# Issuing two weight loads from GpSimd, and taking the attention output's product out of PSUM

## The chip, the cores and the metric

The kernel runs on one core of a Trainium2 chip. The core has a matrix engine (TensorE, "PE" in the profile, with its weight loads as "PEld"), three elementwise engines (VectorE "DVE", ScalarE "ACT", GpSimd "POOL"), a SyncE ("SP") that here only issues DMAs, and 16 DMA engines. Each engine runs its own instructions in the order in which they were issued and waits on semaphores for the others. The metric is the device time of one execution in microseconds (us), and lower is better.

## The reference

Attention over 8 batches, 12 heads, 448 positions and 64 values a head, with normed q and k, and then a gated MLP that mixes over positions:

```python
q_n, k_n = rmsnorm(q, g_q), rmsnorm(k, g_k)
scores = scale * q_n @ k_n.T
attn = exp(scores - max) / (sum(exp) + 1e-09)
x = (attn @ v) laid out as (8, 448, 768)

h = gelu(x @ w_in)                      # w_in is 768 x 1024
u, v = halves of h
v_n = layernorm(v) * g_ln
v_s = w_sg @ v_n + b_sg                 # w_sg is 448 x 448
out = x + (u * v_s) @ w_out             # w_out is 512 x 768
```

w_in and w_out come as 64-bit floats, and the kernel reads their two 32-bit words and builds 32-bit floats out of them on the chip. Most products are done as three 16-bit matmuls: a value is split into a high half (its rounding to f16) and a low half (what is left), and high x high, high x low and low x high are added up. The low half of a value is always "the value minus its high half", so it needs one elementwise subtraction.

## The kernel before

**The order is a plan.** The kernel isn't issued as it is written. Each engine call is recorded as a task on a tape (lines 201 to 232), and a list scheduler (lines 255 to 414) runs through modelled time and puts the tasks into an order for each engine by priority, readiness and modelled cost (lines 135 to 173). A task recorded with `either` (lines 234 to 243) names several engines that could do it; the plan gives it to the one that by its model ends it first (`best`, lines 245 to 253). VectorE and GpSimd share a port to SBUF; the model calls every GpSimd task a user of that port, and of VectorE's tasks those that touch SBUF alone (lines 175 to 182). When the order is written out (`emit`), a GpSimd task of a modelled cost over `LONG` = 500 ns is ordered behind the last VectorE task that used the port (lines 440 to 443). PSUM has eight banks; the plan gives a tile a bank and frees it when the last user of the tile has ended (lines 391 to 396), with at most two of the kind "pv" at once (line 42). All recorded instructions have line 439 in the profile, so they are told apart by their tiles.

**Attention.** 48 pairs of heads are done in 24 units `u` of two pairs (four heads). For a unit, q and k are loaded by four DMAs from SP (`load_qk`), squared and summed (`squares`), normed (`norms`, small GpSimd instructions), scaled and split into halves (`split`, GpSimd by default: products into `qk`, differences into `hl`), and turned by two transposing DMAs from SP into `qt`. `scores` does seven row blocks: matmuls into `s`, a minimum on VectorE (`jk`), an exponential on ScalarE (`ex`), two instructions that take the halves of the exponential apart (`ahl`), and a transposing DMA from SP into `at`. `pv` (lines 873 to 904) multiplies with v in two parts, `e` = 0 of 512 columns and `e` = 1 of 384: 48 parts in all. Small GpSimd instructions (`rx`, `rh`, `rl`) prepare the reciprocals of the sums; matmuls lay them out as `row` in PSUM, ScalarE copies that to SBUF, and the part ends with the lines that the change touches:

```python
894  V.tensor_tensor(out=ps, in0=ps, in1=row, op=ALU.mult)   # in PSUM, in place
899  copy(xh, ps, XH)                                        # ScalarE, high half
900  V.tensor_tensor(out=xl, in0=ps, in1=xh, op=ALU.subtract) # VectorE, low half
```

So the PSUM tile `pv` is held until the low half is done. `xh` and `xl` are the x that the MLP's matmuls (`mv`, `mu`, and the addition of x in `mo`) read.

**Weights.** `weights` (lines 591 to 689) runs beside the first units. It loads w_in in 12 chunks of 512 KB into `raw` (three buffers, line 606), decodes each with five VectorE instructions into `dec` (lines 584 to 589), and loads a further chunk when a buffer comes free, so up to three ahead. The first chunk has no other wait; the others also wait for the task that `HOLD` names (lines 1145 and 1146). After six chunks the half of w_in is scaled and split into `wi`. Then come w_sg (`wsr`), and w_out in 8 chunks of 384 KB into `rawo` (two buffers, line 673), decoded into `wr` and split into `wo_h` and `wo_l`. All these loads are issued by SP, in one queue with the transposes.

**MLP.** `moe(b)` runs one batch behind attention at a lower priority; the first needs w_in, w_sg and w_out, so the MLP of batch 0 can only end when `weights` has.

Of the kernel before, what the change touches and what calls it, by code (L numbers as in the profile page):

```python
# [8 lines left out]
F32 = mybir.dt.float32  # L9
# [6 lines left out]
ALU = mybir.AluOpType  # L16
# [29 lines left out]
NAT, NAH, NQT, NVH, HLB, GV = 2, 3, 2, 4, 3, 3  # L46
NOT, NX, NEX = 2, 6, 2
EXP_SET = "natural_log_exp_and_others"
BACC_KW = dict(dynamic_dma_scratch_size=1024)
# [54 lines left out]
class Tape:  # L104
# [30 lines left out]
    def cost(self, q, op, a, kw):  # L135
# [15 lines left out]
        if q.eng != "S" and "dma" in op:  # L151
            return 700, 4000, None
        if q.eng == "S":
# [47 lines left out]
    def record(self, q, op, a, kw):  # L201
# [11 lines left out]
        self.count += 1  # L213
        if q.eng == "S":
            t.preds |= self.after
# [231 lines left out]
def kernel(  # L447
# [75 lines left out]
    mm = T.matmul  # L523
    ENG = dict(A=A, V=V, G=G)

    def copy(out, in_, on):
# [11 lines left out]
    def two(out, in0, in1, op, on):  # L538
        tape.either(*[(ENG[e], "tensor_tensor", dict(out=out, in0=in0, in1=in1, op=op)) for e in on])

    SSW = 2 * C7
# [38 lines left out]
    def decode(dst, raw, most=None):  # L580

        hi, lo = raw[:, :, 1], raw[:, :, 0]
        di = dst.bitcast(I32)
        V.tensor_scalar(out=di, in0=hi, scalar1=0x7FFFFFFF, scalar2=None, op0=ALU.bitwise_and)
        more = {} if most is None else dict(op1=ALU.max, accum_out=most)
        V.tensor_scalar(out=dst, in0=dst, scalar1=LEAST, scalar2=None, op0=ALU.max, **more)
        V.tensor_scalar(out=di, in0=di, scalar1=3, scalar2=0x3FFFFFF8, op0=ALU.logical_shift_left, op1=ALU.bitwise_and)
        V.scalar_tensor_tensor(out=di, in0=hi, scalar=-0x40000000, in1=di, op0=ALU.bitwise_and, op1=ALU.bitwise_or)
        V.scalar_tensor_tensor(out=di, in0=lo, scalar=29, in1=di, op0=ALU.logical_shift_right, op1=ALU.bitwise_or)

    def weights():
# [10 lines left out]
        def load_raw(j):  # L602
            if j < len(chunks):
                x, t = chunks[j]
                held, tape.after = tape.after, set() if j < RAWF else tape.after
                raws[j] = stage.tile([P, DH, 2], I32, name="raw", bufs=RAWB)
                SP.dma_start(out=raws[j].rearrange("p a b -> p (a b)"),
                             in_=wi_b[t * P:(t + 1) * P, x * 2 * DH:(x + 1) * 2 * DH])
                tape.after = held
# [3 lines left out]
        for x in (1, 0):  # L613
# [13 lines left out]
            for t in range(KT):  # L627
                wh, wl = (wi[:, t, x, n] for n in range(2))
                A.activation(out=wh, in_=dec[t], func=AF.Copy, scale=wsc)
                V.scalar_tensor_tensor(out=wl, in0=dec[t], scalar=wsc, in1=wh, op0=ALU.mult, op1=ALU.subtract)  # L630
                if t % 2:
                    yield
# [8 lines left out]
        for s_ in range(C7):  # L641
            SP.dma_start(out=wsr[s_ // 2][s_ % 2 * HP:(s_ % 2 + 1) * HP],
                              in_=w_sg.rearrange("(p c) s -> c p s", c=C7)[s_])
# [27 lines left out]
        for j in range(2 * FT):  # L671
            t, es = j // 2, slice(j % 2 * EH, (j % 2 + 1) * EH)
            raw = mlp.tile([P, EH, 2], I32, name="rawo", tag="v" + "hl"[j % 2])
            SP.dma_start(out=raw.rearrange("p a b -> p (a b)"),
                         in_=wo_b[t * P:(t + 1) * P, 2 * EH * (j % 2):2 * EH * (j % 2 + 1)])
            wr = mlp.tile([P, EH], F32, name="wr", tag="gt", bufs=NOT)
            decode(wr, raw)
            A.activation(out=wo_h[:, t, es], in_=wr, func=AF.Copy)
            V.tensor_tensor(out=wo_l[:, t, es], in0=wr, in1=wo_h[:, t, es].bitcast(F32), op=ALU.subtract)
            yield  # L680
# [19 lines left out]
    def load_qk(u, qs=None):  # L700
        if u >= NI // NG:
            return
        qs = qs or [SP]
        b, h0 = u // NU, u % NU * 2 * NG
# [10 lines left out]
    def load_v(i):  # L715
# [9 lines left out]
        for h, half, s0, c0, n in ((0, lo, 0, 0, C4), (0, hi, 0, C4, CM), (1, lo, C4, C4, CM), (1, hi, CM, 0, C4)):  # L725
            SP.dma_start(out=vp[half, :, s0 * D:(s0 + n) * D], in_=src[h][:, :, c0 * D:(c0 + n) * D])
        for j in range(GV):
# [69 lines left out]
    def vsplit(i):  # L797
# [5 lines left out]
        A.activation(out=vf, in_=vr, func=AF.Copy, scale=sc)  # L803
        V.scalar_tensor_tensor(out=vl.rearrange("p c d -> p (c d)"), in0=vr, scalar=sc, in1=vf, op0=ALU.mult, op1=ALU.subtract)
        r.update(vh=vh, vl=vl)
# [51 lines left out]
    def rows(e, rh, rl):  # L857
# [7 lines left out]
        if ROWP:  # L865
            return ps
        row = att.tile([P, C4 * P], F32, name="row", bufs=1)[:, 0:n * P]
        scaled(row, ps, 2.0 ** -25, RW)
# [4 lines left out]
    def pv(u, e):  # L873
# [18 lines left out]
        if ROWP:  # L892
            row = rows(e, *r_)
        V.tensor_tensor(out=ps, in0=ps, in1=row, op=ALU.mult)
        if e == 0:
# [3 lines left out]
        copy(xh, ps, XH)  # L899
        V.tensor_tensor(out=xl, in0=ps, in1=xh, op=ALU.subtract)  # L900
        if e == 1:
# [18 lines left out]
    def moe(b, early=False):  # L920
# [151 lines left out]
        for t in range(CM + b % 2):  # L1072
# [28 lines left out]
            for h in range(2):  # L1101
                SP.dma_start(out=om[b % 2, 2 * t + h] if t < CM else om[h, C7 - 1], in_=ot[h * HP:(h + 1) * HP])
        if b % 2 == 1:
# [145 lines left out]
```

## Time and profile before

| | us |
|---|---|
| median of 3 runs (lowest, highest) | 860.91 (857.09, 862.02) |
| the profiled execution's own time | 860.37 |
| its span, first to last instruction | 858.6 |
| outside the span | 1.8 |
| busy in the span: TensorE | 743.0 |
| busy: ScalarE | 722.3 |
| busy: VectorE | 668.2 |
| busy: GpSimd | 304.5 |

The profile shows one execution. "Busy" is the time with an instruction on the engine; an engine idle before an instruction has the instruction or the DMA that released it named. A page shows the span in 40 equal slices (21.5 us each) with a digit for the busy tenths; the view by windows gives the same in us for chosen stretches. The view of waits adds up who waited for whom. The chain is the work that ended last, followed back from the last instruction.

### The profile page before, as it was taken

To read this page: it belongs to the slowest core of one execution; us is meant where nothing else is said; L and a number is where in the kernel's file an instruction comes from. 1 tells how busy PE (TensorE), PEld (TensorE's weight loads), DVE (VectorE), ACT (ScalarE), POOL (GpSimd) and SP (SyncE) were. 2 spreads that over 40 slices of the span, in tenths; PEclk is the share of its full clock that TensorE was granted. 3 is DMA by queue.
4 is the path that set the end of the run, shared out by engine and by line. 5 is a ranking of instruction groups with operands and counts; after the bars stand their busy time and mean duration, and the time that the engine had idled before them with its cause. 6 is when DMAs were issued, how large, how long until landed. Compare 5 with 4: busy or idle time off the path is not lost.

```text
span 858.6 us, 21024 instructions
## 1 busy us (share of the span) xinstructions
PE 743.0 (87%) x7766; PEld 475.1 (55%) x7766; DVE 668.2 (78%) x1691; ACT 722.3 (84%) x1495; POOL 304.5 (35%) x457
## 2 busy tenths in 40 slices
PE   0445568954999979999999999999999999999997
PEld 0223343532675548655765568556855686558557
DVE  6978988889988878977976898878987978574250
ACT  4677879998898999898989999889999999895451
POOL 2543350045534634452444246323435335000000
PEclk9658668966999999999999999999999999999999
DMA  6999999969999998999699979997999699646002
GB/s 165 252 241 195 216 207 199 213 141 200 169 234 218 226 190 166 246 209 166 137 206 225 226 145 226 240 209 134 198 225 218 140 223 200 136 90 143 19 1 74
DMA packets 433944, 155.97 MB, mean 182 GB/s; under 512 B 402545, under 2 KB 427697, under 8 KB 433841
## 3 DMA queue, kind: packets, MB, share of 16 engines
q1 hardware_dynamic: 433840, 154.63, 89.6%
q8 instruction: 61, 1.00, 0.5%
q14 instruction: 43, 0.34, 0.1%
HBM read 43.57 MB, written 11.01 MB: 64 GB/s over the span
## 4 chain that ended last, share of the span: by engine, by line
PE 55%; ACT 17%; DVE 12%; DMA 9%; issue 5%; POOL 1%; SPq 1%; ACTq 0%; DVEq 0%; POOLq 0%
PE pv L439 11%; PE s L439 7%; DMA at<-ahl 6%; ACT ex L439 4%; ACT ahl L439 3%; DVE jk L439 2%; ACT L439 2%; ACT sqk L439 2%; PE row L439 1%; DVE ahl L439 1%; DMA qk<-in_k_dram 1%; ACT vg L439 1%; ACT u L439 1%; ACT vh L439 1%; DVE pv L439 1%
## 5 line engine op out<-in xcount | busy, mean ns | idle before, releaser
L439 DVE TENSOR_SCALAR_CACHE_REDUCE jk<-s 128x448 bf16<-128x448 f32 x336 | 199.0, 615 | 34.8 <-PE s L439 34.4
L439 ACT ACTIVATE ex<-s,nm 128x448 int32<-128x448 f32 x336 | 213.6, 641 | 12.1 <-DVE jk L439 9.8
L439 ACT ACTIVATE ahl<-ex 128x896 f16<-128x896 uint16 x192 | 181.9, 957 | 9.5 <-DMA at<-ahl 8.9
L439 PE MATMUL s<-qt 64*64 64x448 f16 x2016 | 142.8, 375 | 48.4 <-DMA qt<-hl 21.3
L439 PEld LDWEIGHTS <-vh 128*64 128x64 f16 (+2 forms) x1792 | 103.2, 112 | 103.6 <-issue 55.7
L439 PE MATMUL pv<-at,vh 128*64 128x192 f16 (+3 forms) x1536 | 133.0, 275 | 27.6 <-ACT ex L439 12.3
L439 DVE TENSOR_SCALAR ahl<-ex 128x896 f16<-128x896 uint16 x144 | 102.5, 712 | 28.8 <-ACT ex L439 22.7
L439 PEld LDWEIGHTS <-qt 64*64 64x64 f16 x2016 | 64.7, 110 | 94.4 <-issue 52.5
L439 POOL TENSOR_TENSOR hl<-qk,hl 128x896 f16<-128x896 f32 (+2 forms) x69 | 93.7, 1364 | 41.7 <-ACT hl L439 9.7
L439 PEld LDWEIGHTS <-wi 128*128 128x128 f16 x576 | 54.5, 99 | 55.5 <-issue 7.2
L439 POOL TENSOR_TENSOR qk<-qk,ny 128x896 f32<-128x896 f32 x46 | 77.1, 1690 | 14.5 <-DVE ahl L439 7.5
L439 POOL TENSOR_TENSOR qk<-qk,gg 128x896 f32<-128x896 f32 x23 | 48.1, 2093 | 96.0 <-ACT sqk L439 77.4
L439 PEld LDWEIGHTS <-xh 128*128 128x128 f16 (+1 forms) x648 | 49.7, 102 | 47.7 <-issue 20.8
L439 PE MATMUL pv<-at,vl 128*64 128x192 f16 (+3 forms) x768 | 74.0, 273 | 0.0
L439 ACT ACTIVATION_READ_ACCUMULATOR ex<-s,nm 128x1 f32 x336 | 71.6, 213 | 0.0
L439 POOL TENSOR_SCALAR rx<-sums 128x8 f32<-128x8 f32 (+1 forms) x48 | 15.0, 313 | 141.8 <-ACT ex L439 140.3
L439 PEld LDWEIGHTS <-vl 128*64 128x64 f16 (+2 forms) x896 | 56.1, 114 | 12.8 <-issue 0.7
L439 DVE TENSOR_REDUCE ss<-sqk 128x14 f32<-128x896 f32 x48 | 51.8, 1079 | 10.2 <-ACT sqk L439 10.1
L439 DVE TENSOR_TENSOR pv<-pv,row 128x512 f32<-128x512 f32 (+1 forms) x48 | 30.2, 629 | 34.3 <-PE pv L439 34.1
L439 ACT ACTIVATE sqk<-qk 128x896 f32<-128x896 f32 x48 | 45.8, 960 | 3.4 <-DMA qk<-in_k_dram 1.8
L439 PEld LDWEIGHTS <-xl 128*128 128x128 f16 (+1 forms) x408 | 36.6, 102 | 19.5 <-DVE v_i L439 1.1
L439 ACT ACTIVATE xh<-pv 128x512 f16<-128x512 f32 (+1 forms) x48 | 26.2, 547 | 24.4 <-DVE pv L439 23.7
(1104 smaller groups left out, 1799.7 us busy)
## 6 DMA issues: line engine op xcount, KB each, us to landing
qk<-in_q_dram SPq DMA_DIRECT2D x48, 224.0 KB, 3.9
qk<-in_k_dram SPq DMA_DIRECT2D x48, 224.0 KB, 4.7
out_dram<-ot SPq DMA_DIRECT2D x56, 192.0 KB, 3.4
raw<-in_moe_w_in_dram SPq DMA_DIRECT2D x12, 512.0 KB, 5.4
vr<-in_v_dram SPq DMA_DIRECT2D x32, 192.0 KB, 4.2
vr<-in_v_dram SPq DMA_DIRECT2D x32, 144.0 KB, 3.7
rawo<-in_moe_w_out_dram SPq DMA_DIRECT2D x8, 384.0 KB, 3.6
at<-ahl SPq DMA_TRANSPOSE x168, 4.6
```

The costliest lines, as they stand in the source:

```text
L439: ins = getattr(q.nc_eng, op)(*first, *a, **kw)
```

## The change

Two things change, and the rest of the diff gives names to choices that keep their old values (`DEC`, `VL`, `WL`, `SQ_`, `VQ`, `KQ`, `XQ` leave their instructions where they were).

First, the 12 loads of w_in and the 8 of w_out are issued by GpSimd's queue instead of SP's. The plan's model takes a DMA on GpSimd as 1100 ns of GpSimd (it had 700, which nothing used) and 4000 ns until it lands, and such a DMA heeds the hold as SP's do.

Second, the product of the attention output goes to a new SBUF tile `sx`, which shares its two buffers with `row` (that had one). The high half is copied from there, and the subtraction for the low half reads SBUF alone, so that GpSimd can do it as well: the plan picks VectorE or GpSimd.

```diff
+DEC, XL, VL, WL = 'V', 'VG', 'V', 'V'
+RQ, OQ, SQ_, VQ, GLAT, KQ, XQ = 'G', 'G', 'S', 'S', (1100, 4000), 'S', 'S'
...
         if q.eng != "S" and "dma" in op:
-            return 700, 4000, None
+            return *GLAT, None
...
-        if q.eng == "S":
+        if "dma" in op:
             t.preds |= self.after
...
+    LD = dict(S=SP, G=G, A=A)
...
+    def stt(out, in0, by, in1, op0, op1, on):
+        tape.either(*[(ENG[e], "scalar_tensor_tensor", dict(out=out, in0=in0, scalar=by, in1=in1, op0=op0, op1=op1)) for e in on])
...
                 raws[j] = stage.tile([P, DH, 2], I32, name="raw", bufs=RAWB)
-                SP.dma_start(out=raws[j].rearrange("p a b -> p (a b)"),
+                LD[RQ].dma_start(out=raws[j].rearrange("p a b -> p (a b)"),
...
             raw = mlp.tile([P, EH, 2], I32, name="rawo", tag="v" + "hl"[j % 2])
-            SP.dma_start(out=raw.rearrange("p a b -> p (a b)"),
+            LD[OQ].dma_start(out=raw.rearrange("p a b -> p (a b)"),
...
-        row = att.tile([P, C4 * P], F32, name="row", bufs=1)[:, 0:n * P]
+        row = att.tile([P, C4 * P], F32, name="row", bufs=2 if "G" in XL else 1)[:, 0:n * P]
...
-        V.tensor_tensor(out=ps, in0=ps, in1=row, op=ALU.mult)
+        if "G" in XL:
+            sx = att.tile([P, C4 * P], F32, name="sx", tag="row", bufs=2)[:, 0:n * P]
+            V.tensor_tensor(out=sx, in0=ps, in1=row, op=ALU.mult)
+            ps = sx
+        else:
+            V.tensor_tensor(out=ps, in0=ps, in1=row, op=ALU.mult)
...
         copy(xh, ps, XH)
-        V.tensor_tensor(out=xl, in0=ps, in1=xh, op=ALU.subtract)
+        two(xl, ps, xh, ALU.subtract, XL)
```

`two` (lines 538 and 539) is `either` over the named engines with one `tensor_tensor`. Since the plan is made anew, the order of everything behind these edits may differ too.

More of the change, by code (lines that the diff above doesn't have):

```diff
@@ L588, in decode @@
         V.scalar_tensor_tensor(out=di, in0=hi, scalar=-0x40000000, in1=di, op0=ALU.bitwise_and, op1=ALU.bitwise_or)
-        V.scalar_tensor_tensor(out=di, in0=lo, scalar=29, in1=di, op0=ALU.logical_shift_right, op1=ALU.bitwise_or)
+        stt(di, lo, 29, di, ALU.logical_shift_right, ALU.bitwise_or, DEC)
     def weights():
@@ L629, in weights @@
                 A.activation(out=wh, in_=dec[t], func=AF.Copy, scale=wsc)
-                V.scalar_tensor_tensor(out=wl, in0=dec[t], scalar=wsc, in1=wh, op0=ALU.mult, op1=ALU.subtract)
+                stt(wl, dec[t], wsc, wh, ALU.mult, ALU.subtract, WL)
                 if t % 2:
@@ L641, in weights @@
         for s_ in range(C7):
-            SP.dma_start(out=wsr[s_ // 2][s_ % 2 * HP:(s_ % 2 + 1) * HP],
+            LD[SQ_].dma_start(out=wsr[s_ // 2][s_ % 2 * HP:(s_ % 2 + 1) * HP],
                               in_=w_sg.rearrange("(p c) s -> c p s", c=C7)[s_])
@@ L702, in load_qk @@
             return
-        qs = qs or [SP]
+        qs = qs or [LD[KQ if u else "S"]]
         b, h0 = u // NU, u % NU * 2 * NG
@@ L725, in load_v @@
         for h, half, s0, c0, n in ((0, lo, 0, 0, C4), (0, hi, 0, C4, CM), (1, lo, C4, C4, CM), (1, hi, CM, 0, C4)):
-            SP.dma_start(out=vp[half, :, s0 * D:(s0 + n) * D], in_=src[h][:, :, c0 * D:(c0 + n) * D])
+            LD[VQ].dma_start(out=vp[half, :, s0 * D:(s0 + n) * D], in_=src[h][:, :, c0 * D:(c0 + n) * D])
         for j in range(GV):
@@ L803, in vsplit @@
         A.activation(out=vf, in_=vr, func=AF.Copy, scale=sc)
-        V.scalar_tensor_tensor(out=vl.rearrange("p c d -> p (c d)"), in0=vr, scalar=sc, in1=vf, op0=ALU.mult, op1=ALU.subtract)
+        stt(vl.rearrange("p c d -> p (c d)"), vr, sc, vf, ALU.mult, ALU.subtract, VL)
         r.update(vh=vh, vl=vl)
@@ L1101, in moe @@
             for h in range(2):
-                SP.dma_start(out=om[b % 2, 2 * t + h] if t < CM else om[h, C7 - 1], in_=ot[h * HP:(h + 1) * HP])
+                LD[XQ if b < B - 1 else "S"].dma_start(out=om[b % 2, 2 * t + h] if t < CM else om[h, C7 - 1], in_=ot[h * HP:(h + 1) * HP])
         if b % 2 == 1:
```

## The prediction

> **What bounds the kernel now.** I read the engines' totals and the slices first, then two windows, then the waits of TensorE.
>
> ```profile
> PE 743.0 (87%) x7766; PEld 475.1 (55%) x7766; DVE 668.2 (78%) x1691; ACT 722.3 (84%) x1495; POOL 304.5 (35%) x457
> ...
> PE   0445568954999979999999999999999999999997
> ...
> DVE  6978988889988878977976898878987978574250
> ...
> PEclk9658668966999999999999999999999999999999
> ```
>
> The slices show two regimes. In the first ten (0 to 215 us) TensorE is half idle, its granted clock is low, and VectorE is the fullest engine. From then on TensorE is full to the end. The windows give that in us (columns: window, length, then busy us and instructions of PE, PEld, DVE, ACT and POOL, granted clock, DMA share, GB/s):
>
> ```profile
> 0.00:210.00 210.00, 111.11 (x1138) 63.45 (x1140) 177.33 (x438) 166.49 (x327) 77.20 (x114) 0.75 0.94 203
> 210.00:859.00 649.00, 631.90 (x6636) 411.68 (x6628) 490.82 (x1253) 555.83 (x1169) 227.31 (x343) 0.99 0.89 175
> ```
>
> TensorE idles 210 - 111.1 = 98.9 us before 210 us and only 649 - 631.9 = 17.1 us after. So an edit pays in the first window, where it lets work reach TensorE sooner, and afterwards by at most what it takes out of 17.1 us. VectorE is 177.3 / 210 = 84% busy in the first window and the DMA engines 94%: two candidates for what paces it. The chain of waits through the first 215 us mixes them:
>
> ```profile
> by line: DMA at<-ahl 12.1%; PE pv L439 11.3%; issue 8.7%; ACT ahl L439 8.1%; ACT ex L439 5.8%; DMA qk<-in_k_dram 4.4%; DVE dec L439 3.5%; ACT sqk L439 3.5%; DVE jk L439 3.5%; SPq L439 3.1%; ACT L439 3.0%; DMA qt<-hl 2.9%; PE s L439 2.2%; AC
> ```
>
> No engine holds it alone; the transposes `at<-ahl` are its largest single item, 12.1% of 215 us = 26 us.
>
> **The change part by part.** I work from the profiled execution, 858.6 us of span and 1.8 around it, 860.4 in all; the median shown is 0.5 above.
>
> *The low half.* The first window holds eight of the 48 subtractions:
>
> ```profile
> L439 DVE TENSOR_TENSOR xl<-pv,xh 128x512 f16<-128x512 f32 x4 | 2.7, 687 | 0.0
> ...
> L439 DVE TENSOR_TENSOR xl<-pv,xh 128x384 f16<-128x384 f32 x4 | 2.2, 553 | 0.7 <-ACT xh L439 0.7
> ```
>
> That is 4.9 us of VectorE. The model makes GpSimd's version about twice as dear (1162 against 602 ns for 512 columns by lines 169 and 173), so the plan gives it away only when over half a us of work stands ahead on VectorE. At 84% load I take five of eight, worth 5 x 0.62 = 3.1 us. Bounds: nothing, if VectorE isn't what is late, and 4.9. On GpSimd the nearest instructions are subtractions of the same shapes:
>
> ```profile
> 29.75 1.15 POOL L439 TENSOR_TENSOR hl<-qk,hl 128x512 f16<-128x512 f32 x1 [0.35 <-POOL hl L439]
> 31.47 0.92 POOL L439 TENSOR_TENSOR hl<-qk,hl 128x384 f16<-128x384 f32 x1 [0.56 <-DVE ahl L439]
> ```
>
> So a moved one ends about 0.45 us later for the matmuls that read it, and GpSimd gets some 5 us in a window where it idles 210 - 77 = 133. It adds waits: the moved subtraction sits behind VectorE's last port user, and behind it on GpSimd stand the norms and reciprocals; and the product of the next part needs the buffer of `sx`. How far apart are the parts?
>
> ```profile
> L439 DVE TENSOR_TENSOR pv<-pv,row x48: 550/626/700, 62.7 to 801.6; 128x512 f32<-128x512 f32 x24, 128x384 f32<-128x384 f32 x24
> ```
>
> 48 products (durations least, median and most in ns) in 739 us, 15 us apart on the mean, which covers the second wait; without that cover `jk` would queue behind a product on VectorE. After 210 us VectorE is 491 of 649 us busy with TensorE full, so the other 40 subtractions cost and bring nothing.
>
> *The bank.* `pv` is now free when the product is done, and no longer after the high and low halves. Where did TensorE wait for a low half?
>
> ```profile
> PE ms__4409 L439 <- DVE xl L439: 4.8, 1, 4.8
> ...
> PE mo__7939 L439 <- DVE xl L439: 0.8, 1, 0.8
> ...
> PE s L439 <- DVE xl L439: 0.3, 1, 0.3
> PE mv__898 L439 <- DVE xl L439: 0.2, 1, 0.2
> ```
>
> 6.1 us in all. The long one, at 303 us, reads no x (`ms` multiplies w_sg), so it waited for the bank:
>
> ```profile
> 302.74 0.70 DVE L439 TENSOR_TENSOR pv<-pv,row 128x512 f32<-128x512 f32 x1
> ...
> 305.39 1.63 DVE L439 TENSOR_TENSOR vl<-vg,vh 128x512 f16<-128x512 f32 x3 [1.43 <-ACT vh L439]
> 306.09 0.58 ACT L439 ACTIVATE xh<-pv 128x512 f16<-128x512 f32 x1
> ...
> 306.94 0.68 DVE L439 TENSOR_TENSOR xl<-pv,xh 128x512 f16<-128x512 f32 x1
> ```
>
> The product ended at 303.4, the low half at 307.6. With the bank gone at 303.4, what is late next is the rest of `vl`, ready at 307.0: TensorE could start `ms` but soon runs out. I take 3 us for the part; bounds 0 (a new plan may place a like wait elsewhere) and 6.1. The high half now reads SBUF instead of PSUM:
>
> ```profile
> 63.47 0.60 ACT L439 ACTIVATE xh<-pv 128x512 f16<-128x512 f32 x1 [2.64 <-DVE pv L439]
> ...
> 217.30 0.62 ACT L439 ACTIVATE hl<-qk 128x512 f16<-128x512 f32 x1
> ```
>
> The second is the same copy out of SBUF: 0.02 us more, 48 times, is 1 us of ScalarE over the run, which I cost at nothing under TensorE; if it all showed, 1 us.
>
> *SP's queue.* Twenty loads leave it. They cost it 12 x 0.53 and 8 x 0.47 = 10.1 us of issue, and waits for their buffers at its head:
>
> ```profile
> L439 SPq DMA_DIRECT2D raw<-in_moe_w_in_dram x12: 327/532/1240, 7.2 to 99.9; - x12
> ...
> L439 SPq DMA_DIRECT2D rawo<-in_moe_w_out_dram x8: 333/468/582, 150.2 to 198.2; - x8
> ...
> SPq L439 <- DVE dec L439: 6.0, 5, 2.6
> ...
> SPq L439 <- DVE wr L439: 5.4, 5, 1.9
> ```
>
> Behind them stood transposes. Two show it on the chain:
>
> ```profile
> 62.07 3.50 SPq L439 DMA_DIRECT2D raw<-in_moe_w_in_dram  x2
> 65.63 2.28 SPq L439 DMA_TRANSPOSE at<-ahl  x1
> ...
> at<-ahl SPq DMA_TRANSPOSE x168, 4.6
> ...
> qt<-hl SPq DMA_TRANSPOSE x48, 4.4
> ...
> 29.43 6.32 DMA qt<-hl
> ...
> 65.63 7.83 DMA at<-ahl
> ```
>
> Against the medians these were 7.83 - 4.6 = 3.2 and 6.32 - 4.4 = 1.9 us late, each with loads of `raw` just ahead. The bytes still cross the same 16 engines, so I take 2 us of 5.1, with 0 and 5.1 as bounds.
>
> *GpSimd's queue.* An issue on GpSimd is in no row. Below stands 0, since it can hide in 133 us of idle time; above, GpSimd's longest regular instruction, 2.08 us (below), for each of 20, that is 42. I take 0.53, as on SP, and hide it. Not hidden is the first chunk: it has no wait, and on GpSimd it can start before q and k of unit 0 have landed, where SP sent it after them:
>
> ```profile
> 2.88 4.61 DMA qk<-in_k_dram
> ...
> 7.23 0.59 SPq L439 DMA_DIRECT2D raw<-in_moe_w_in_dram  x1
> ```
>
> 512 KB at the window's 203 GB/s is 2.6 us; bounds 0 and 2.6, and I take 1 us of loss. The second and third chunk, held until the first transposes, also move ahead of the loads of v and of unit 2; their bytes are the same, and I count nothing.
>
> Sum: 860.4 - 3.1 - 3 - 2 + 1 = 853.3; I say **853.5**.
>
> **The rivals.** *The transfers pace the start.* With the DMA engines at 94% and the same bytes, VectorE's relief turns into idle time, and the bank's wait is placed elsewhere: 860.4 - 2 + 1 = 859.4. For it: `at<-ahl` leads the chain. Against it are VectorE's waits for DMAs in that window, 3.0 us in all:
>
> ```profile
> DVE ahl L439 <- DMA at<-ahl: 2.7, 2, 1.7
> ...
> DVE dec L439 <- DMA raw<-in_moe_w_in_dram: 0.3, 1, 0.3
> ```
>
>
> *The plan leaves the low half on VectorE.* Its model prices it lower there; then 3.1 is lost: 856.4.
>
> *The queue moves its waits to GpSimd, and the kernel gets slower.* The 6.0 + 5.4 = 11.4 us for `dec` and `wr` now stand at GpSimd's head, with the reciprocals and the q and k of the next unit behind them. TensorE has waited for those:
>
> ```profile
> PE row L439 <- POOL rh L439: 11.9, 1, 11.9
> ```
>
> If all 11.4 reach TensorE and the plan, now off, gains nothing at the bank: 860.4 + 11.4 - 3.1 - 2 + 1 = 867.7. It decides once a load waits longer than GpSimd idles before its next instruction anyway, 133 / 114 = 1.2 us on the mean; the longest of the waits above were 2.6 and 1.9. For it: one queue, in order. Against: GpSimd is 37% busy there.
>
> *Descriptor writing and VectorE shut each other out.* The trace shows the shared port:
>
> ```profile
> 32.34 2.08 POOL L439 TENSOR_TENSOR qk<-qk,gg 128x896 f32<-128x896 f32 x1
> ...
> 32.50 2.40 DVE L439 TENSOR_SCALAR ahl<-ex 128x896 f16<-128x896 uint16 x1 [0.57 <-ACT ex L439]
> ...
> 47.65 0.63 DVE L439 TENSOR_SCALAR ahl<-ex 128x896 f16<-128x896 uint16 x1 [1.06 <-DMA at<-ahl]
> ```
>
> The same `ahl` took 2.40 us against 0.63 because it could end only with GpSimd's instruction, 1.77 lost. If each of 20 issues cost VectorE between 0 and 1.77, at 84% load the loss is 0 to 30 us; a third of that, as the issue is short beside 2.08, is 10: 853.3 + 10 = 863.5. Of such a lock the Trainium skill speaks against this change: the page "SBUF — State Buffer", section "SBUF: two separate sides", says that a DMA from GpSimd's queue has its descriptors written by GpSimd, which can't write them while VectorE runs an instruction that takes both ports, and gives 620 ns alone against 3100 beside one. By it 20 loads would land some 2.5 us later each, an estimate from that page. The lock agrees with the row of 2.40; its effect on a load is in no run here. Three chunks in flight would hide such a delay for w_in.
>
> **How the numbers follow.** Forecast 0.55, transfers 0.20, low half left 0.08, GpSimd's queue 0.11, the lock 0.06. All terms at their best give 860.4 - 4.9 - 6.1 - 5.1 = 844.3, and the slow rival 867.7: the range, rounded, is 843.5 to 867.5. A measurement of this kernel tells about 0.5% (4.3 us) from no change, so faster means under 856.6 and slower over 865.2. Faster: forecast 0.53, half of the third case 0.04, together 0.57. Same: 0.20 + 0.04 + 0.02 of the forecast + 0.02 of the lock = 0.28. Slower: 0.11 + 0.04 = 0.15.
>
> **What would show it.** Right: TensorE's idle time before 210 us falls from 98.9 by 4 to 6; some 20 of 48 `xl` stand on GpSimd at about 1.15 and 0.92; no wait of an `ms` for `xl`; SP no longer waits for `dec` and `wr`. Wrong: `qk` of unit 0 lands over 2 us later; GpSimd waits for `dec` before `rh` or `qk` while TensorE waits for `row` or `s`; `ahl` and `dec` on VectorE grow in the mean; or the second window, which should keep its 632 us of TensorE, grows because the new plan mixes the matmuls otherwise. That last I can't price from any row, and it is what I fear most.

## The result and the profile after

The changed kernel takes 871.5 us in the median of six runs (868.79 to 875.09), the kernel before 860.74 (857.09 to 862.02) beside it: ratio 1.0132, 95% interval [1.011, 1.0154]. It is slower by 1.3%, and 4 us above the range of the prediction. The profiled execution took 874.79 us, 873.0 of them in the span.

The page of the changed kernel, totals and two of the rows of 40 slices (21.8 us each):

```profile
PE 748.3 (86%) x7766; PEld 475.5 (54%) x7766; DVE 674.1 (77%) x1701; ACT 714.9 (82%) x1481; POOL 330.4 (38%) x481
...
PE   0323576974999999999999999999999999999997
...
DVE  5576877899989789878987896878988878675250
```

The first four digits of TensorE fell from 0445 to 0323. TensorE, VectorE and ScalarE have little more work or less (GpSimd, which is never full, has 26 us more); something that all of them wait for is late. Two windows, in the columns of the prediction (length, then busy us and instructions of PE, PEld, DVE, ACT, POOL, clock, DMA share, GB/s):

```profile
0.00:210.00 210.00, 112.46 (x1080) 60.77 (x1081) 162.39 (x407) 151.31 (x296) 82.63 (x119) 0.75 0.94 188
210.00:873.00 663.00, 635.88 (x6686) 414.69 (x6685) 511.73 (x1295) 563.58 (x1186) 247.82 (x363) 0.99 0.89 176
```

The first window is as long as before, but VectorE did 177.3 - 162.4 = 14.9 us less in it and ScalarE 166.5 - 151.3 = 15.2 less, and TensorE 1080 of its matmuls instead of 1138. What wasn't done by 210 us is done behind it: the second window has 663 us instead of 649, all of the 14.4 us by which the span grew. The loss arises in the start and is then carried to the end, where TensorE is full.

Two places in the start. First the timeline of GpSimd and TensorE (start, duration, then the wait before it), and TensorE's row before:

```profile
1.54 0.72 POOL L441 DMA_DIRECT2D raw<-in_moe_w_in_dram  x1
...
25.68 4.60 PE L441 MATMUL s<-qt 64*64 64x448 f16 x62 [25.68 <-DMA qt<-hl]
```

```profile
21.26 4.87 PE L439 MATMUL s<-qt 64*64 64x448 f16 x62 [21.26 <-DMA qt<-hl]
```

The first matmul starts 4.4 us later. The first chunk of w_in now starts at 1.54 instead of 7.23 and runs beside q and k of unit 0; the chain of waits puts 7.44 us on the load of q behind it:

```profile
1.58 7.44 DMA qk<-in_q_dram
...
25.65 10.03 DMA vr<-in_v_dram
```

The second row is the same effect a little later: chunks 2 to 4 are issued from 23.94 to 25.54 us and run beside the loads of v. The last of these lands 10.03 us after its issue; before, the same four loads took 5.0 to 5.3 us each.

Second, three windows of 5 us, after and then before:

```profile
55.00:60.00 5.00, 0.00 (x1) 0.00 (x0) 4.87 (x10) 4.26 (x10) 1.64 (x3) 0.50 1.31 118
60.00:65.00 5.00, 0.00 (x0) 0.00 (x0) 1.10 (x5) 0.00 (x0) 1.50 (x5) 0.50 1.25 95
65.00:70.00 5.00, 0.47 (x6) 0.49 (x8) 0.76 (x2) 0.48 (x1) 0.00 (x0) 0.50 1.26 109
```

```profile
55.00:60.00 5.00, 2.56 (x24) 2.03 (x26) 4.20 (x9) 5.00 (x10) 2.94 (x4) 0.50 1.19 262
60.00:65.00 5.00, 3.88 (x52) 2.67 (x48) 2.26 (x4) 2.36 (x7) 0.00 (x0) 0.78 1.17 282
65.00:70.00 5.00, 2.15 (x38) 1.36 (x38) 5.00 (x19) 5.00 (x12) 2.30 (x3) 1.00 0.78 143
```

From 60 to 70 us nearly every engine stands, and the DMA engines have work (the share can pass 1, and did before too, with SP's queue alone) but move some 100 GB/s where they moved 282 and 143. What they carry there is `at<-ahl` from SP and `raw` from GpSimd: two transposes issued at 51.04 and 57.12 land 18.4 and 15.8 us later, two chunks issued beside them at 51.37 and 59.91 land 17.8 and 12.8 us later, and TensorE stands for 14.5 us up to 69.5. The first product of the attention output, `sx` on VectorE, then starts at 74.66 us, 11.9 later than before (62.7), where the first matmul was 4.4 late. The landing times say the same (least, median, most, first of `raw`, then of `at`; before 3.5/5.4/8.1 and 3.4/4.6/7.8):

```profile
DMA to landing us min/median/max: 4.0/7.2/17.8
...
DMA to landing us min/median/max: 3.4/4.5/18.4
```

Of the low halves, 45 of 48 stayed on VectorE:

```profile
L441 DVE TENSOR_TENSOR xl<-sx,xh x45: 498/684/2206, 83.5 to 816.8; 128x384 f16<-128x384 f32 x23, 128x512 f16<-128x512 f32 x22
```

And the waits for buffers, at SP's head before, now stand at GpSimd's:

```profile
POOL rawo L441 <- DVE wr L441: 17.2, 3, 7.6
...
POOL raw L441 <- DVE dec L441: 6.0, 3, 4.2
```

### The profile page after: what moved, and what is told of

It reads as the page before. It is cut to its first block, busy times and chain, and to the rows that moved or that the text cites. A ratio compares the mean times of both kernels' runs of the same rounds, so it can differ in the third digit from the quotient of the medians.

```text
span 873.0 us, 21063 instructions
## 1 busy us (share of the span) xinstructions
PE 748.3 (86%) x7766; PEld 475.5 (54%) x7766; DVE 674.1 (77%) x1701; ACT 714.9 (82%) x1481; POOL 330.4 (38%) x481
## 4 chain that ended last, share of the span: by engine, by line
PE 52%; DVE 19%; ACT 10%; issue 8%; DMA 8%; POOL 2%; SPq 0%; DVEq 0%; ACTq 0%; POOLq 0%
PE pv L441 10%; PE s L441 7%; DVE jk L441 4%; DMA at<-ahl 4%; ACT ex L441 2%; DVE ahl L441 2%; DVE dec L441 2%; ACT ahl L441 2%; DVE ss L441 2%; DVE hl L441 1%; DMA rawo<-in_moe_w_out_dram 1%; PE row L441 1%; DVE wr L441 1%; DMA vr<-in_v_dram 1%; ACT vh L441 1%
## 5 line engine op out<-in xcount | busy, mean ns | idle before, releaser
L441 ACT ACTIVATE ex<-s,nm 128x448 int32<-128x448 f32 x336 | 212.1, 635 | 17.2 <-DVE jk L441 15.9
L441 ACT ACTIVATE ahl<-ex 128x896 f16<-128x896 uint16 x186 | 175.6, 952 | 22.3 <-DMA at<-ahl 21.8
L441 PE MATMUL pv<-at,vh 128*64 128x192 f16 (+3 forms) x1536 | 131.3, 273 | 25.2 <-issue 15.8
L441 DVE TENSOR_SCALAR ahl<-ex 128x896 f16<-128x896 uint16 x150 | 106.1, 708 | 30.2 <-ACT ex L441 25.7
L441 POOL TENSOR_TENSOR qk<-qk,ny 128x896 f32<-128x896 f32 x46 | 77.5, 1695 | 29.2 <-DVE dec L441 13.8
L441 POOL TENSOR_TENSOR qk<-qk,gg 128x896 f32<-128x896 f32 x24 | 50.2, 2093 | 76.4 <-ACT sqk L441 59.3
L441 POOL TENSOR_SCALAR rx<-sums 128x8 f32<-128x8 f32 (+1 forms) x48 | 20.1, 420 | 122.7 <-ACT ex L441 121.0
L441 PEld LDWEIGHTS <-vl 128*64 128x64 f16 (+2 forms) x896 | 55.3, 112 | 13.8 <-DVE vl L441 1.2
L441 DVE TENSOR_REDUCE ss<-sqk 128x14 f32<-128x896 f32 x48 | 51.8, 1079 | 13.1 <-ACT sqk L441 13.0
L441 DVE TENSOR_TENSOR sx<-pv,row 128x512 f32<-128x512 f32 (+1 forms) x48 | 29.7, 619 | 35.2 <-PE pv L441 35.2
L441 ACT ACTIVATE xh<-sx 128x512 f16<-128x512 f32 (+1 forms) x48 | 27.9, 581 | 26.1 <-DVE sx L441 26.0
```

Of the source, the lines that this page charges most:

```text
L441: ins = getattr(q.nc_eng, op)(*first, *a, **kw)
```

## The experiments

The expectations name theories by letters. P: the new plan is worse whatever the loads do. Q: loads on a second queue beside SP's transposes make both crawl. H: a load that waits for its buffer at GpSimd's head holds up what stands behind it. D: GpSimd's writing of descriptors and VectorE shut each other out. Later come I (issuing on GpSimd costs), R (the room for its descriptors), S (the software queue's transfers share the DMA engines badly) and W (the loads only run at other times).

**e1, e2: which half of the change.** e1 is the changed kernel with the loads on SP, e2 the changed kernel with the low half named for VectorE alone, which brings back the product in PSUM.

```diff
-RQ, OQ, SQ_, VQ, GLAT, KQ, XQ = 'G', 'G', 'S', 'S', (1100, 4000), 'S', 'S'
+RQ, OQ, SQ_, VQ, GLAT, KQ, XQ = 'S', 'S', 'S', 'S', (1100, 4000), 'S', 'S'
```

> The changed kernel with all 20 weight loads back on SP's queue; only the product in SBUF and the free choice for the low half stay. Theory Q (loads on a second queue run beside SP's transposes, and both crawl): the loss of 10.8 us is gone, 857 to 863 us, ratio to before within 0.995 to 1.003, and no transpose over 9 us before 80 us. Theory P (the new plan is worse by itself, through the product in SBUF): still 866 to 873.

```diff
-DEC, XL, VL, WL = 'V', 'VG', 'V', 'V'
+DEC, XL, VL, WL = 'V', 'V', 'V', 'V'
```

> The changed kernel with the product back in PSUM and the low half on VectorE alone; only the 20 loads on GpSimd's queue stay. Theory Q: the whole loss stays, 868 to 876 us, with transposes of over 9 us and loads of w_in of over 12 us before 80 us. Theory P: most of the loss is gone, 858 to 865.

e1: 860.29 us, ratio 0.9994 [0.9974, 1.0013]. e2: 871.67, 1.012 [1.0063, 1.0178]. The loads carry the whole loss. The product in SBUF shows no gain; the plan of e1 left all 48 low halves on VectorE, so the move of a low half itself was hardly tried.

**e3, e4: the plan or the queue.** e3 keeps the plan of before and sends the 20 loads to another engine only when the order is written out; e4 keeps the changed kernel's plan and sends them to SP (without the order behind the shared port that GpSimd's tasks get).

```diff
+                eng = q.nc_eng
+                if op == "dma_start" and kw["out"].tensor.name.split(".")[0] in ('raw', 'rawo'):
+                    eng = tc.nc.gpsimd          # e4: tc.nc.sync;  e8: tc.nc.scalar
-                ins = getattr(q.nc_eng, op)(*first, *a, **kw)
+                ins = getattr(eng, op)(*first, *a, **kw)
```

> The kernel before with its plan untouched: TensorE, VectorE and ScalarE run the very same instructions in the same order; only when the order is written out, the 20 loads are given to GpSimd instead of SP, at the same place in the plan, with no wait behind VectorE's port. Theory Q: slower by 6 to 14 us with long transposes where loads fall beside them. Theory P: 858 to 864, no loss. Theory H (a load waiting at GpSimd's head for its buffer holds up norms and reciprocals): slower by 4 to 12 us, with transposes of usual length and TensorE waiting for rh, rl or qt that GpSimd delivered late.

> The changed kernel with its plan untouched, but the 20 loads written out to SP's queue at their place in the plan, and without the order behind VectorE's last port instruction. Theory Q: 858 to 864 us, the first TensorE instruction may stay late by some 4 us since the first chunk still stands ahead, no transpose over 9 us. Theory P: still 868 to 874. Theory H: 858 to 864, with GpSimd's waits for dec and wr (23 us) gone.

e3: 877.24, 1.0201 [1.017, 1.0233]. e4: 864.13, 1.0042 [1.0024, 1.0061]. With TensorE, VectorE and ScalarE in the very order of before, the loads on GpSimd cost more than the change did. The new plan by itself costs 0.4%, with the first matmul late there too, since it puts the first chunk early.

**e5, e6, e7: which loads.** As e3, with the first chunk alone, chunks 2 to 12, or w_out alone on GpSimd.

```diff
+                    seen += tile_ == "raw"
+                    if tile_ == "raw" and seen == 1:   # e6: seen > 1;  e7: tile_ == "rawo"
+                        eng = tc.nc.gpsimd
```

> The plan of before; of the 20 loads only the first chunk of w_in goes to GpSimd, which has it out at 2 us instead of 7. Theory Q splits in two parts, and this is the first: the chunk shares the engines with q and k of unit 0, the first matmul comes 3 to 4 us later (21.3 before, 24.7 in the run with all 20), and the time is 2 to 4 us longer, 862.5 to 865. If the late start is hidden further on, it is 859.5 to 862.

> The plan of before; chunks 2 to 12 of w_in go to GpSimd, the first one and w_out stay with SP. Theory Q: this is the main part, 868 to 875 us, with a pair of qt transposes of about 11 us at 30 us and a run of at transposes of about 3 us each (20 us for six) by 50 us; the first matmul at 21.3 as before. Theory H: the same time but with transposes as before.

> The plan of before; only the 8 loads of w_out go to GpSimd. Fewer transposes lie between 150 and 200 us, so theory Q says a small loss, 861 to 865 us. Theory H: the waits for wr (6.8 us in the run with all 20) stand at GpSimd's head ahead of the preparation of unit 6, 863 to 868, with TensorE waiting for qt or rh after 180 us. A gain (under 858) would make this the version to keep.

e5: 865.33, 1.0063 [1.0045, 1.0082]. e6: 870.73, 1.0124 [1.0104, 1.0143]. e7: 867.23, 1.0096 [1.0075, 1.0118]. Each group costs, and they sum to more than e3; perhaps a delay that one causes partly covers the next, which no run shows.

**e8: another second queue.** As e3, with `tc.nc.scalar`.

> The plan of before; all 20 loads are issued by ScalarE, whose queue the hardware serves as it does SP's: again a queue beside that of the transposes, but without descriptors written by GpSimd. Theory Q: transposes of 3 us each and more while loads are under way, and 870 to 880 us (some 10 us of ScalarE's time for the issues are in it). Theory D (GpSimd and VectorE shut each other out while descriptors are written): transposes and landings as before, and 860 to 868.

858.76, 0.998 [0.9956, 1.0004]. Twenty loads from ScalarE's queue, beside the same transposes, cost nothing. Q in its general form falls: a second queue need not cost. The timelines of e3 and then of e8, rows of GpSimd or ScalarE and of SP:

```profile
23.04 2.07 POOL L442 TENSOR_TENSOR qk<-qk,gg 128x896 f32<-128x896 f32 x1 [7.37 <-DVE dec L442]
...
26.77 3.34 POOL L442 TENSOR_TENSOR qk<-qk,ny 128x896 f32<-128x896 f32 x2
30.05 0.67 POOL L442 DMA_DIRECT2D raw<-in_moe_w_in_dram  x1
...
32.86 1.10 POOL L442 DMA_DIRECT2D raw<-in_moe_w_in_dram  x2
...
32.94 11.71 SPq L442 DMA_TRANSPOSE qt<-hl  x2
```

```profile
24.68 0.33 ACTq L442 DMA_DIRECT2D raw<-in_moe_w_in_dram  x1
25.08 0.42 ACTq L442 DMA_DIRECT2D raw<-in_moe_w_in_dram  x1
27.86 0.34 ACTq L442 DMA_DIRECT2D raw<-in_moe_w_in_dram  x1
...
31.40 5.87 SPq L442 DMA_TRANSPOSE qt<-hl  x2
```

The row of a transpose is SP's time for issuing it; it lands later. The landings of this pair, in the kernel before, e3 and e8:

```profile
DMA to landing us min/median/max: 4.3/6.8/9.3
```

```profile
DMA to landing us min/median/max: 12.3/13.5/14.6
```

```profile
DMA to landing us min/median/max: 4.2/5.7/7.1
```

From ScalarE, chunks 2 to 4 are issued 3.5 us and more before the two transposes of q and k, which land 7.1 and 4.2 us after their issue; from GpSimd, where the multiplications of unit 1 stand ahead of the chunks in the queue from 23.04 to 30.05, they are issued just before and with the pair, which lands after 14.6 and 12.3. (Before, with the loads ahead of them on SP, after 9.3 and 4.3.) The changed kernel has no such meeting at 30 us; its own are the two places shown above.

**e9, e10, e11: what GpSimd could do to them.** All with the order of before. e9 is e3 with four times the room for descriptors, e10 is e3 with five buffers for `raw`, and e11 leaves the loads on SP and was meant to add a small one on GpSimd beside each.

```diff
-BACC_KW = dict(dynamic_dma_scratch_size=1024)
+BACC_KW = dict(dynamic_dma_scratch_size=4096)
```

> The kernel of e3 (order of before, all 20 loads issued from GpSimd; ratio 1.0201 there) with one number changed: dynamic_dma_scratch_size, the room that the program reserves for the descriptors of GpSimd's queue, is 4096 bytes instead of 1024. Theory R (the room is too small, so GpSimd's loads wait for one another): ratio at most 1.010, longest landing of raw back from 13 or more to under 9 us, GpSimd's issues shorter. Every other theory (S: the software queue's transfers and SP's transposes share the DMA engines badly; I: issuing on GpSimd itself costs; H: a load waiting for its buffer at GpSimd's head holds up what stands behind it): 1.016 to 1.023, landings as in e3.

```diff
+                if tl.kw.get("name") == "raw":
+                    tl.kw["bufs"] = 5
```

> The kernel of e3 with five buffers for raw instead of three, in the same order, so that a load of w_in no longer waits for VectorE's decoding of the chunk three before it (5.1 us of such waits at GpSimd's head in e3). The loads of w_out keep their buffers. Theory H: those waits go, and with them about half of the loss: ratio 1.008 to 1.014, first chain of pv products after 100 us earlier by 3 us or more than in e3. S, I and R: 1.016 to 1.024; under S rather more, since more loads then stand beside the transposes.

```diff
+                    spare = real_pools["const"].tile([128, 1], mybir.dt.int32, name="spare%d" % self.spares)
+                    tc.nc.gpsimd.dma_start(out=spare, in_=kw["in_"][:, 0:1])
```

> The kernel before, its 20 loads on SP as ever, and beside each of them one more load issued from GpSimd at the same place: 128 rows of 4 bytes into a tile of its own that nothing reads and that waits for nothing. It has the issue and the 128 rows of a real load without its bytes and without its buffer wait. Theory I (GpSimd's issue and descriptor writing cost, whatever is carried): ratio 1.008 to 1.02. S (the bytes of the software queue beside the transposes) and H (the buffer waits): 0.998 to 1.004. R would show in part: the room is used as much, but the loads are gone sooner.

e9: 878.29, 1.0227 [1.02, 1.0255]. e10: 878.19, 1.0238 [1.021, 1.0266]. e11: 859.83, 1.0008 [0.9989, 1.0026]. R falls. H falls for w_in: without those waits the kernel is no faster, and the longest landing of `at` rose from 10.0 to 15.2 us. For w_out, whose buffers are other tiles' too, it wasn't tried. e11 says nothing on I and D: its page has no load from GpSimd and as many instructions on GpSimd as before, where e3 has 20 more and a queue of software descriptors. First e11, then e3:

```profile
PE 741.9 (86%) x7766; PEld 475.0 (55%) x7766; DVE 668.4 (78%) x1691; ACT 721.6 (84%) x1495; POOL 303.8 (35%) x457
```

```profile
PE 742.4 (85%) x7766; PEld 474.6 (54%) x7766; DVE 670.2 (77%) x1691; ACT 722.4 (83%) x1495; POOL 316.3 (36%) x477
...
q0 software_dynamic: 2368, 9.44, 4.2%
```

The added lines ask for a tile named `raw` behind the line that has put the real tile, of another name, in its place, so they never act; e11 is the kernel before, measured once more. What the other runs say of I and D: VectorE's 1691 instructions took 670.2 us in e3 and 670.3 in e8, where GpSimd issues nothing, so GpSimd's issues did not lengthen them; the issues of w_in took 0.53 to 0.98 us each in e3; and in e5 a single one of 0.7 us comes with a loss of 5.4. That VectorE kept descriptors from being written, out of sight of these rows, isn't excluded.

**e12: the changed kernel on ScalarE's queue.** `RQ, OQ = 'A', 'A'`, planned anew.

> The changed kernel, product in SBUF and choice of engine for the low half kept, with the 20 loads planned for and issued from ScalarE instead of GpSimd. If the loss belongs to GpSimd's queue alone, as e8 says, what is left is the plan's own: 0.997 to 1.006 (e4 1.0042, e1 0.9994), raw landing at 5 to 6 us in the median and at most 10. If a plan that frees SP's queue is bad wherever the loads go, over 1.008. Faster than 0.995 only if the parts that e1 and e8 show at nothing help each other; I do not expect it.

884.34, 1.0301 [1.0282, 1.0321], far over the 1.008 from which a plan that frees SP's queue was to be called bad. The waits of TensorE up to 110 us show where:

```profile
PE s L441 <- DMA qt<-hl: 35.9, 1, 35.9
```

The first matmul comes at 35.9 us instead of 21.26. In this plan VectorE decodes the first chunk ahead of the sums of squares of unit 0, and its chain of waits runs over that load (8.15 us). Landings of `raw` are ordinary (5.8 us in the median), the longest of `at` is 13.4. So much of this loss is the plan's (its order with the loads on SP wasn't run), and a plan made anew is no clean test of a queue.

**e13: the transfers by themselves.** Behind the last output of the kernel before, short phases with nothing else running, four times over.

```diff
+        for kind in ("tN", "tS", "tA", "tG", "tQ", "oS", "oA", "oG", "lN", "lA", "lG"):
+            nc.vector.tensor_scalar(out=flat[:, 0:8], in0=last[:, 0:8, 0], scalar1=0, scalar2=None, op0=ALU.mult)
...
+                    on[e].dma_start(out=raw[:, c:c + step], in_=wi_b[0:P, c:c + step])
...
+                    nc.sync.dma_start_transpose(out=at[:, :, c * P:(c + 1) * P], in_=flat)
```

> The kernel before, and behind its last output eleven short phases, four times over, each begun by one small VectorE instruction and ended when all its transfers have landed; no other work stands beside them. Phases t: four transposes of 128x1792 as those of the attention, on SP's queue, alone (tN) or with one 512 KB load of w_in queued ahead of them on SP (tS), or started at the same time from ScalarE (tA), from GpSimd (tG), or from GpSimd as two loads of half the row each (tQ). Phases o: the load alone from SP, ScalarE, GpSimd. Phases l: two loads of 224 KB on SP, alone (lN) or beside the 512 KB load from ScalarE (lA) or GpSimd (lG). Theory S (the software queue's bytes and SP's transposes share the DMA engines badly): the load alone takes about the same from all three (within 1 us), but the last transpose of tG lands at least 2 us later than that of tA, or the load of tG at least 3 us later than that of tA. Its rival W (nothing is wrong with the queues, the loss is that the loads run at other times): tA and tG agree within 1 us, transposes and load. The whole time means nothing here; it grows by the phases.

Its DMA issues, with the median us to landing last, and then VectorE's timeline of the second round, where each row begins the next phase:

```profile
ldoS<-in_moe_w_in_dram SPq DMA_DIRECT2D x4, 512.0 KB, 4.0
ldoA<-in_moe_w_in_dram ACTq DMA_DIRECT2D x4, 512.0 KB, 3.5
ldoG<-in_moe_w_in_dram POOLq DMA_DIRECT2D x4, 512.0 KB, 3.8
...
trtN<-src SPq DMA_TRANSPOSE x16, 3.8
trtS<-src SPq DMA_TRANSPOSE x16, 4.5
trtA<-src SPq DMA_TRANSPOSE x16, 5.1
trtG<-src SPq DMA_TRANSPOSE x16, 6.2
```

```profile
945.36 0.17 DVE L1228 TENSOR_SCALAR src<-ldlG 128x8 f16<-128x8 int32 x1 [2.14 <-DMA ldlG<-in_moe_w_in_dram]
954.67 0.17 DVE L1228 TENSOR_SCALAR src<-ldlG 128x8 f16<-128x8 int32 x1 [9.13 <-DMA trtN<-src]
966.14 0.17 DVE L1228 TENSOR_SCALAR src<-ldtS 128x8 f16<-128x8 int32 x1 [11.29 <-DMA trtS<-src]
977.76 0.17 DVE L1228 TENSOR_SCALAR src<-ldtA 128x8 f16<-128x8 int32 x1 [11.45 <-DMA trtA<-src]
989.00 0.17 DVE L1228 TENSOR_SCALAR src<-ldtG 128x8 f16<-128x8 int32 x1 [11.07 <-DMA trtG<-src]
```

The rows begin the phases tN, tS, tA, tG and tQ, so their distances are the phases' lengths: 9.3, 11.5, 11.6 and 11.2 us. Over the four rounds four transposes take 9.0 to 9.3 us alone, 11.4 to 11.6 with the load ahead of them on SP, 11.6 to 11.8 with it from ScalarE and 11.2 to 11.3 with it from GpSimd (13.1 in the first round): no queue wastes the engines' time. The median landings, 4.5, 5.1 and 6.2 us, look as if a load beside a transpose delayed it more than one ahead of it. But they count from each transpose's issue, and SP issues the four at other times. Counted from the beginning of the phase (issue plus landing, second round), they land at

| | 1st | 2nd | 3rd | 4th |
|---|---|---|---|---|
| alone (tN) | 3.8 | 5.7 | 7.4 | 9.1 |
| load ahead on SP (tS) | 6.5 | 8.1 | 9.8 | 11.3 |
| load from ScalarE (tA) | 6.5 | 8.1 | 9.8 | 11.5 |
| load from GpSimd (tG) | 6.6 | 7.9 | 9.4 | 11.1 |

So one load costs each transpose some 2 to 3 us, from whichever queue. S falls here by its own number: the last transpose of tG lands no later than that of tA (1.2 us later in the first round, where S asked for 2). W's 1 us holds for the transposes but for that round, and is just missed by the load, 5.8 us to landing from GpSimd and 4.6 from ScalarE. Nor do these phases show the crawl of the kernels: they have one load beside four transposes, e3 and e16 three beside two. (tQ issued four quarters of the row, not two halves, and took 12.5 to 13.8 us.)

**e14, e15, e16, e17: the same loads at other times.** The 12 loads of w_in alone. e14 leaves them at their places on GpSimd. e15 and e17 move each ahead of up to two GpSimd instructions and hold the first until g_q has landed; e17 has a larger tile for that holding copy. e16 puts them on ScalarE, and late: the first to the front, each other behind up to five instructions.

```diff
-        for t in self.schedule():
+        for t in self.moved(list(self.schedule())):
...
+            while past < 2:                       # e16: forward, past < 5, until a task reads the tile
+                x = order[j - 1]
+                if x in loads or x.eng == "V" and n >= 5 and self.reads(x, loads[n - 5]):
+                    break
+                j -= 1
+                past += x.eng == "G" and x.occ > 100
+            order.insert(j, order.pop(i))
...
+                        hold = real_pools["const"].tile([1, 1], F32, name="hold")    # e17: [1, 32]
```

> Order of before, the 12 loads of w_in issued from GpSimd at their places in the plan, those of w_out left on SP: the control for e15. From e5 (first chunk alone, 1.0063) and e6 (the other eleven, 1.0124) both theories expect 1.012 to 1.02.

> As e14, still GpSimd's queue, at other times. The first load stands behind a GpSimd copy of one element of g_q, so that it starts once g_q has landed, near the 7.2 us at which SP issues it in the kernel before (2.3 us in e14); each other load is moved ahead of up to two GpSimd instructions that stood before it, with five buffers for raw, so that it starts nearer to SP's times (26.8 us for the second to fourth; e3 had 30.1 to 33.9, beside the transposes of q and k that SP issues at 29.4). Theory W (what costs is that the loads run at other times): at most 1.006. Theory S (the software queue itself): within 0.003 of e14.

> The 12 loads of w_in from ScalarE's queue (with w_out's as well this cost nothing in e8, 0.998), at times like GpSimd's: the first moved to the front of its queue (about 2 us instead of 7.5), each other behind up to five more ScalarE instructions, so that the second to fourth start at 28 to 34 us beside the transposes of q and k instead of 24.7 to 27.9. Theory W: 1.006 or more, with the first matmul at 23 us or later. Theory S: 0.997 to 1.003.

> As e15 with one size changed: the tile that the holding copy writes has 128 bytes in its partition instead of 4. In e15 the transposes were slower to the very end, long after the last load (after 500 us median 4.7 us to landing, shortest 3.9, against 3.9 and 3.4 before), which nothing of a load's time can do; what else e15 changed is that every tile behind the 4 bytes lies 4 bytes further. If that is it, the landings after 500 us come back to 3.9 to 4.2, and the ratio says what e15 was meant to: theory W (the times) at most 1.006, theory S (the software queue itself) 1.010 to 1.016 as e14. If the landings stay at 4.7, the addresses are not the cause and e15's question stays open.

e14: 871.36, 1.0133 [1.0104, 1.0163]. e16: 871.59, 1.0136 [1.0105, 1.0168]. The queue that cost nothing in e8 loses as much in all as GpSimd's when its loads run late. The timeline of e16, ScalarE's and SP's rows, and the landings of the pair:

```profile
29.00 0.33 ACTq L469 DMA_DIRECT2D raw<-in_moe_w_in_dram  x1
30.75 1.35 ACTq L469 DMA_DIRECT2D raw<-in_moe_w_in_dram  x2
...
29.53 10.19 SPq L469 DMA_TRANSPOSE qt<-hl  x2
...
DMA to landing us min/median/max: 12.4/13.0/13.6
```

With the loads beside them the transposes of q and k land after 13.6 and 12.4 us, as they did from GpSimd. (e16 leaves w_out's loads on SP and e8 doesn't; up to 150 us, where these begin, that makes no difference.) The first load went out at 5.5 us and not at 2, and the first matmul was on time (21.33), so that part of the expectation wasn't tried.

e15: 888.36, 1.0323 [1.03, 1.0346]. e17: 890.82, 1.035 [1.0323, 1.0377]. Both far off every expectation, and for another reason: the transposes of the attention stay slow long after the last load. Landings of `at` after 500 us, before and then e17:

```profile
DMA to landing us min/median/max: 3.4/3.9/6.8
```

```profile
DMA to landing us min/median/max: 3.9/4.7/7.5
```

The runs' starts can still be compared. This table, worked out from VectorE's timelines, has the start of the n-th of the 48 products `pv<-pv,row` against the kernel before (us; + is later):

| in the kernel before at | e3 | e6 | e7 | e8 | e14 | e15 | e16 | e17 | e18 |
|---|---|---|---|---|---|---|---|---|---|
| 62.7 | +5.8 | +2.3 | -2.1 | -2.4 | +5.5 | +0.9 | +4.8 | +5.6 | -0.3 |
| 110.7 | +7.0 | +7.5 | -2.2 | -6.0 | +8.9 | +3.4 | +4.4 | +5.9 | -2.7 |
| 215.2 | +10.4 | +8.2 | +5.2 | -5.1 | +9.3 | +5.0 | +4.2 | +6.4 | -3.0 |
| 801.6 | +12.9 | +10.8 | +9.8 | -3.1 | +9.8 | +29.2 | +11.5 | +26.9 | -2.2 |

Each column is one execution. e7 has the order of before up to 150 us and still is 2.1 us ahead at 62.7, so differences of some 2 us tell nothing. Up to 110.7 us, the end of w_in's loads, the other times cut the loss of e14 from 8.9 to 3.4 and 5.9 us although the transposes were slower; on ScalarE they turned 6.0 us of gain into 4.4 of loss. So the times carry some 3 to 5 of the 9 us that w_in costs by then. Whether GpSimd's queue adds something at equal times stays open, since e15 and e17 were spoiled for it. e16's last 7 us came only after 215 us, in two steps: TensorE waits 2.1 us up to 369 and 2.1 in two pieces up to 639 us, and in the 10 us behind each the granted clock is 0.83 and 0.84 where it was 1.00 at these places before. What brings the two waits is open.

**e18: a version to beat both.** As e8, with five buffers and each load of w_in from the second on ahead of up to three ScalarE instructions.

> The version that might beat both: as e8 (order of before, 20 loads from ScalarE's queue, 0.998), with five buffers for raw and each load of w_in from the second on moved ahead of up to three ScalarE instructions. Theory W: the loads stand further from the transposes that wait behind them; 0.992 to 1.0. If the times near 25 us are already right and the gain at 215 us is given back later, as in e8, 0.996 to 1.002. If an earlier load stands beside the transposes before it instead, over 1.003.

858.6, 0.9976 [0.9961, 0.9992]. Some 2 us faster than before, by half of what a measurement of this kernel was taken to tell; e8 was the same. Against the changed kernel it is 1.5% faster (0.9976 against 1.0132).

## Why the prediction was wrong

The forecast was 853.5 us; the kernel takes 871.5. Point by point:

- **The step that failed** is the one on GpSimd's queue: "their bytes are the same, and I count nothing" for the loads that move, and 1 us for the first chunk. The bytes were the same and their time wasn't. A load on SP stands ahead of the transposes or behind them. On GpSimd it starts when GpSimd's own order comes to it. In the changed kernel that put chunks 2 to 4 beside the loads of v (10.03 us on the chain) and two further chunks beside transposes of the attention, which then landed after 18.4 and 15.8 us while TensorE stood for 14.5; in e3 it put chunks 2 to 4 beside the transposes of q and k. With the order of before, chunks 2 to 12 cost 1.24% = 10.7 us (e6), w_out 0.96% = 8.3 (e7). The first chunk delayed the first matmul by 4.4 us in the changed kernel and by 24.35 - 21.26 = 3.1 in e5, where it costs 0.63% = 5.4 alone (in the trace of e5 the products are 1.5 us late at 215.2 and 4.5 at 801.6, so part of the cost comes much later, as in e16); the bound of 2.6 took the load's bytes for the delay.
- **The price of an issue** was nearly right: 0.58 us in the median for w_in and 0.56 for w_out, for the 0.53 taken. That it hides wasn't tried by itself.
- **SP's queue.** The 2 us may have been the right size, but for another queue: e8 takes the loads off SP and is 0.2% faster, 1.7 us, with an interval that takes in no change, and e18 2.1. (The 1.9 us of lateness read from the chain were too few: that transpose, issued at 29.43, landed 9.3 us later, and the row of 6.32 ends before.)
- **The low half and the bank**, 3.1 and 3 us, show no gain together: e1 has 0.9994. The plan moved 3 of 48 low halves, not 20. For what remains, the product in SBUF and the bank freed early, the rival of the transfers gave a reason beforehand that fits, though no run tried it alone: VectorE isn't what is late in the first window. Its "DMA engines at 94%" is no proof of that: the share passes 1 in windows of the kernel before (1.19, 1.17).
- **The rival "the queue moves its waits to GpSimd"** ended nearest, 867.7 (a time that the range, rounded to 867.5, left out), by another mechanism. The waits did move, 17.2 us for `wr` and 6.0 for `dec` at GpSimd's head, but with the waits for `dec` gone the kernel was no faster (e10, 1.0238 against 1.0201).
- **The lock**, whose 853.3 + 10 is 863.3 and not 863.5, didn't cost VectorE what was priced: its instructions took the same time with the issues on GpSimd (e3) as with those on ScalarE (e8). The other way round, the Trainium skill ("SBUF — State Buffer", section "SBUF: two separate sides") would put the late landings down to VectorE's instructions. In the windows from 60 to 70 us VectorE was busy for 1.9 of 10 us, and the loads crawled there, which speaks against it; no run tried it.
- **"The new plan mixes the matmuls otherwise"**, the fear without a price, has one: 0.42% = 3.6 us (e4), with the first matmul at 24.2 us because that plan puts the first chunk early on SP too.

What is shown: the loads carry the loss (e1, e2), not by the room for descriptors (e9) or w_in's buffer waits (e10), and other times alone put the product of 110.7 us back by 10.4 us on a queue that otherwise cost nothing (e16 against e8). What is only argued: that the times are all of it on GpSimd, and what share of w_out's 0.96% is GpSimd's wait for `wr`. Why transfers crawl when they meet is open; e13 didn't bring it about. Against the times alone stands that stretches of 5 us with a share over 1.1 at 120 GB/s or less, among those between 25 and 125 us, were seen only with loads on GpSimd: three each in the changed kernel and e10, two each in e2 and e9, one in e6; but none in e3, e14, e15 or e17, which have them there as well. The line at 120 is drawn by hand: e14 has 131 at the lowest, e12 and e16 on ScalarE 135 and 157, and e1 on SP 145.

## What to carry to other kernels

Moving a DMA to another engine's queue moves it in time: before pricing the issue, find what will stand ahead of it in the new queue, and which transfers it will then run beside. Three loads issued 3.5 us and more ahead of a pair of transposes let them land after 7.1 and 4.2 us, and issued with the pair after 13.6 and 12.4 (e8, e16); a single load made no such difference (e13), so try it at the size that the kernel has. When a planner rewrites the order, take the edits apart with the old order held fixed, or the plan's own 0.4% (e4), and much of the 3% of e12, is read as the queue's. And look in the trace for what an edit was to add before its time is read: e11's 1.0008 was the time of an unchanged program.

## What the hardware showed unasked

- With nothing else running, a 512 KB load delays the first of four transposes from 3.8 to between 6.3 and 6.6 us behind the start of the phase, whether it is queued ahead on SP or comes from ScalarE or GpSimd (e13).
- The Trainium skill ("DMA: Bandwidth & Descriptors", section "Issuing engines are not separate DMA queues") says that transfers interleave on the same engines whoever issues them, and that several issuers save only the time of issuing. The phases of e13 agree: 11.2 to 11.8 us from three queues (apart from one of 13.1). Whole kernels don't, 0.998 and 1.0201 (e8, e3), where the issuing engine's order also set when a load ran, chunk 2 at 24.68 and at 30.05 us.
- Two kernels in which one more tile of 4 or of 128 bytes moves every later tile by 32 or 128 bytes had slower transposes throughout, 4.7 us in the median after 500 us instead of 3.9, and lost 24 and 21 us more behind 215 us (e15, e17). Five buffers (e10) and GpSimd's loads (e14) don't do that. So the tiles' addresses are suspected, which no run tried alone: in the kernel before, the sources and targets of the transposes start at multiples of 256 bytes.
